# Float64 weights brought to two TensorE floats: a shift-and-or and a subtraction in place of three matrix products

## The chip, the cores and the metric

One core of a Trainium2 chip runs the kernel. The metric is device microseconds of one execution, on that core. [...] The other engines named here are VectorE (DVE), ScalarE (ACT), GpSimd (POOL) and SyncE (SP), whose queue issues all loads and stores.

## The reference, cut to what matters

```python
# attention: 8 batches, 8 heads, 576 positions, 64 per head
scores = where(0 <= rel < 128, q @ k.T / 8 + bias, -1e9)
x = softmax(scores) @ v                  # -> (8, 576, 512)
# gated layer: w_in (512, 1024), w_spatial (576, 576), w_out (512, 512)
h = maximum(x @ w_in, 0); u, v = halves(h)
v = layer_norm(v)
v_s = einsum('ts,bsd->btd', w_spatial, v) + b_spatial
out = (u * v_s) @ w_out
```

`w_in` and `w_out` arrive as float64, 8 bytes an element.

## The kernel before, in words

**The work.** Everything that follows is one program of one core, written out instruction by instruction. Attention of the first batch is done in fp32: `raw_tile` (scores of one 128-query tile of a head pair, and their exponentials), `raw_sums`, `raw_out` (scaling, transposes on TensorE, product with v). Attention of the batches 1 to 7 is done per head pair by `products` (P), `scores` (C), `values_split` (V) and `attention` (A). The gated layer of a batch has 5 v units (four of 128 positions and a remainder, `v_rem`), 8 u units, 8 s units (the spatial product) and 8 o units (the output product), each of 8 to 14 matmuls into one of two PSUM banks, tag "m". Nearly all TensorE time goes to these units; each factor stands as a high and a low part, so a product is three matmuls.

**The weights.** A 128-row piece of `w_in` has two halves of 512 columns: half 1 feeds the v units, half 0 the u units. With four pieces each, and four of `w_out`, 12 pieces go through `split_w64` (L386). A piece is loaded as int32 pairs, low and high word. L399 (ACT) takes the high word's absolute value as a float, L403 clamps it, L407 shifts its exponent and upper 20 fraction bits into the fp32 place, L411 puts sign and top exponent bit back: the result `x` holds the upper 20 fraction bits. `copy` makes the high part, an fp32r cast of `x`. L419 cuts the power of two out of `x`, and L423 multiplies the low word, as an unsigned number, by it. For the eight pieces of `w_in` (`WPE` True) TensorE then forms `x` minus high minus (minus low word) with three products by a unit matrix and by its negative (`ident`, `minus`; L441, L442, L443) in a bank of tag "m", and a second `copy` takes that to the low part. For `w_out` (`WPE` False) two DVE operations, L431 and L435, do the same. Each `split_w64` has two scratch tiles, of tag "gs" or "vraw".

**The order.** `record` adds units to a `Plan`; `copy`, `relu` and some scalings may go to ACT or DVE, the rest names its engine. The plan works out an order from weights, due times and data, and writes it out, so each engine has one fixed order in which it waits for what it needs. The string `OPENING` sets in which order the first units are recorded, and so who waits for which buffer: `a` and `w` are the pieces of half 1 and half 0, `z` those of `w_out`, `X`, `x`, `Y`, `y`, `g` the spatial weights, `t`, `m`, `n` batch 0's attention, `L`, `P`, `C`, `V`, `A` later attention, `v`, `u`, `s`, `o` the gated layer. 64 matmuls on a tile of ones (L362) run in between at the start.

**The place that matters below.** The first s unit needs all v parts of batch 0 (L910 and, of the remainder, L940). After the first two s units both "m" banks are taken until L979 has multiplied an s result into u.

Of the kernel before, what the change touches and what calls it, by code (L numbers as in the profile page):

```python
# [26 lines left out]
CLAMP = _as_f32((1150 << 20) | 0xFFFFF)  # L27
TINY = _as_f32(897 << 20)
# [165 lines left out]
def attn_gmlp_kernel(ctx, tc, qk, v, w_in, w_spT, b_sp, w_out, outT):  # L194
# [9 lines left out]
    DM, DF = w_in.shape  # L204
    DH = DF // 2
# [10 lines left out]


    WTMP = ("vraw", 3)
    WPE = (True, True, False)
    OPENING = (  # L220
# [40 lines left out]
    def pe(*cols):  # L261
        return sum(12 + n / 2.38 for n in cols)
# [27 lines left out]

    rstat = fixed([P, 2, 4, 2 * NP], F32, "rstat")
    ident = fixed([P, P], F32, "ident")
    minus = fixed([P, P], F32R, "minus")

    def parts(b, a, z, step=P, key=()):

# [12 lines left out]
    def constants():  # L309
# [35 lines left out]

        def f():
            nc.vector.tensor_scalar(ident(), diag()[:, :P], 0.0, None, ALU.is_equal)
            nc.vector.tensor_scalar(minus(), ident(), -1.0, None, ALU.mult)
        plan.add("DVE", 290, 500, f, [(diag, 0)], [(ident, 0), (minus, 0)])
# [36 lines left out]
    def split_w64(src, dst, tmp, hi, lo, due, on_pe, late=()):  # L386

        n = src[1]  # L390
        ta, tx = tmp
        low = lambda: src[0]()[:, :, 0]
        high = lambda: src[0]()[:, :, 1]
        a, x, ai, xi = ta, tx, lambda: ta().bitcast(I32), lambda: tx().bitcast(I32)
        part, PART = (late[0], (late[0], 0)) if late else (lo, (dst[0], (*dst[1], 1)))
        A, X, W, HI, LO = (ta, 0), (tx, 0), (src[0], 0), (dst[0], (*dst[1], 0)), (dst[0], (*dst[1], 1))

        def f():
            nc.scalar.activation(a(), high().bitcast(F32), AF.Abs)  # L399
        plan.add("ACT", act(n) + 100, due, f, [W], [A])  # L400

        def f():
            nc.vector.tensor_scalar(a(), a(), TINY, CLAMP, ALU.max, ALU.min)  # L403
        plan.add("DVE", dve(n, True), due, f, [A], [A])

        def f():
            nc.vector.tensor_scalar(xi(), ai(), 0x07FFFFFF, 3, ALU.bitwise_and, ALU.logical_shift_left)  # L407
        plan.add("DVE", dve(n, True), due + 1, f, [A], [X])
# [4 lines left out]
        def top():  # L413
            copy(n, lambda: (hi(), x()), due + 3, [X], [HI], fast=True)
        if on_pe and not late:
            top()

        def f():
            nc.vector.tensor_scalar(ai(), xi(), -0x800000, None, ALU.bitwise_and)  # L419
        plan.add("DVE", dve(n, True), due + 4, f, [X, A], [A])  # L420

        def f():
            nc.vector.scalar_tensor_tensor(part() if on_pe else a(), low().bitcast(U32), -2.0 ** -52 if on_pe else 2.0 ** -52, a(),  # L423
                                           ALU.mult, ALU.mult)
        plan.add("DVE", dve(n), due + 5, f, [A, W], [PART] if on_pe else [A])
        if late or not on_pe:
            top()
        if not on_pe:

            def f():  # L430
                nc.vector.tensor_tensor(x(), x(), hi().bitcast(F32), ALU.subtract)  # L431
            plan.add("DVE", dve(n), due + 6, f, [X, HI], [X])

            def f():
                nc.vector.tensor_tensor(lo(), x(), a(), ALU.add)  # L435
            plan.add("DVE", dve(n), due + 7, f, [X, A], [LO])
            return
        pt = plan.buf(ps, "m", 2, [P, 512], F32)

        def f():  # L440
            nc.tensor.matmul(pt()[:, :n], ident(), x(), start=True, stop=False)  # L441
            nc.tensor.matmul(pt()[:, :n], minus(), hi(), start=False, stop=False)  # L442
            nc.tensor.matmul(pt()[:, :n], minus(), part(), start=False, stop=True)  # L443
        plan.add("PE", pe(4 * n, n, n) + 130, due + 6, f, [PART, X, HI, (ident, 0), (minus, 0)], [(pt, 0)])
        copy(n, lambda: (lo(), pt()[:, :n]), due + 7, [(pt, 0)], [LO])

    def win_load(half, c, due, tag, bufs):
        st = plan.buf(work, tag, bufs, [P, DH, 2], I32)
# [670 lines left out]
```

## Time and profile before, and how to read it

| | |
|---|---|
| median of 3 runs | 565.38 us (562.99 to 565.69) |
| the profiled execution | span 563.3 us from its first to its last instruction; the page gives no other time of it |
| busy PE, DVE, ACT | 550.4 (98%), 463.5 (82%), 420.0 (75%) us |
| chain that ended last | PE 13% of the span, nothing else over 0.5% |
| L441, L442, L443 together | 24 product instructions on 8 pieces, between 16 and 65 us |
| POOL | 30.1 us busy (5%) |

The span of the profiled execution lies 2.1 us under the median and 0.3 us over the fastest run. A busy time is the union of an engine's instructions; successive instructions of DVE and ACT overlap by a little in the records, so what one costs its queue is the time from its start to the next one's start.

### The profile page before, as it was taken

To read this page: it belongs to the slowest core of one execution; us is meant where nothing else is said; L and a number is where in the kernel's file an instruction comes from. 1 tells how busy PE (TensorE), PEld (TensorE's weight loads), DVE (VectorE), ACT (ScalarE), POOL (GpSimd) and SP (SyncE) were. 2 spreads that over 40 slices of the span, in tenths; PEclk is the share of its full clock that TensorE was granted. 3 is DMA by queue.
4 is the path that set the end of the run, shared out by engine and by line. 5 is a ranking of instruction groups with operands and counts; after the bars stand their busy time and mean duration, and the time that the engine had idled before them with its cause. 6 is when DMAs were issued, how large, how long until landed. Compare 5 with 4: busy or idle time off the path is not lost. (4 is left out here: it accounts for less than half of the span.)

```text
span 563.3 us, 16409 instructions
## 1 busy us (share of the span) xinstructions
PE 550.4 (98%) x6184; PEld 474.8 (84%) x6184; DVE 463.5 (82%) x1756; ACT 420.0 (75%) x1329; POOL 30.1 (5%) x75
## 2 busy tenths in 40 slices
PE   8999997999999999999999999999999999999997
PEld 4566786888989899998989989998989989888987
DVE  6999999999999999868988897989988898625340
ACT  5999985988898889757886775887977787634321
POOL 0000010000100010001100020001000010001000
PEclk8999998999999999999999999999999999999999
DMA  7937414877668857575167644487267523410002
GB/s 234 365 126 261 110 44 95 214 186 185 132 136 185 154 130 169 121 184 139 43 154 170 170 115 93 117 176 182 80 147 173 129 43 70 90 44 23 1 1 84
DMA packets 131028, 74.28 MB, mean 132 GB/s; under 512 B 109314, under 2 KB 121602, under 8 KB 130948
## 3 DMA queue, kind: packets, MB, share of 16 engines
q1 hardware_dynamic: 130948, 73.23, 52.8%
q8 instruction: 48, 0.79, 0.6%
q14 instruction: 32, 0.26, 0.2%
HBM read 37.13 MB, written 9.44 MB: 83 GB/s over the span
## 5 line engine op out<-in xcount | busy, mean ns | idle before, releaser
L971 PE MATMUL m<-wsp,vn 128*128 128x288 f16 x768 | 112.6, 289 | 0.0
L950 PE MATMUL m<-xt,win 128*128 128x288 f32 x768 | 110.6, 298 | 0.3
L715 ACT ACTIVATE prob<-prob,stat 128x192 f32<-128x192 f32 (+2 forms) x252 | 107.2, 430 | 2.9 <-DVE stat L709 2.7
L950 PEld LDWEIGHTS m<-xt,win 128*128 128x128 f32 x768 | 104.0, 188 | 2.9 <-ACT vt L383 0.8
L997 PE MATMUL m<-gs,wout 128*128 128x288 f32 x732 | 101.8, 297 | 0.0
L997 PEld LDWEIGHTS m<-gs,wout 128*128 128x128 f32 x732 | 97.9, 188 | 0.8 <-issue 0.2
L744 ACT ACTIVATE pq<-prob,stat 128x192 f16<-128x192 f32 (+2 forms) x252 | 90.0, 428 | 6.2 <-DVE stat L738 4.1
L899 PE MATMUL m<-win,xt 128*128 128x512 f32 x384 | 92.0, 393 | 0.1
L971 PEld LDWEIGHTS <-vn 128*128 128x128 f16 x768 | 72.6, 99 | 20.6 <-issue 0.2
L749 DVE SCALAR_TENSOR_TENSOR pq<-prob,stat,pq 128x192 f16<-128x192 f32 (+2 forms) x252 | 86.8, 390 | 2.5 <-ACT pq L744 2.3
L899 PEld LDWEIGHTS m<-win,xt 128*128 128x128 f32 x384 | 71.0, 188 | 15.3 <-issue 0.5
L709 DVE CUSTOM_DVE_ANT_0 prob<-s,tabs 128x192 f32<-128x192 f32 (+2 forms) x252 | 71.0, 330 | 3.0 <-PE s L695 2.8
L979 DVE SCALAR_TENSOR_TENSOR u<-m,rows,u 128x288 f32<-128x288 f32 x64 | 32.8, 514 | 25.0 <-PE m L971 24.2
L715 ACT ACTIVATION_READ_ACCUMULATOR prob<-prob,stat 128x1 f32 x252 | 48.3, 192 | 0.0
L695 PE MATMUL s<-qkraw 64*64 64x192 f32 (+1 forms) x1008 | 44.0, 310 | 0.0
L379 ACT CAST gs<-u 128x288 fp32r<-128x288 f32 x48 | 20.5, 426 | 30.3 <-DVE u L979 30.1
L827 PEld LDWEIGHTS <-vh 64*64 64x64 f16 x1232 | 34.7, 107 | 9.3 <-issue 6.2
L827 PE MATMUL x<-pt,vh 64*64 64x192 f16 (+2 forms) x1232 | 39.6, 224 | 1.8 <-POOL am L836 1.8
L873 POOL TENSOR_TENSOR st<-st,nhalf 128x1 f32<-128x1 f32 (+1 forms) x40 | 26.0, 649 | 235.1 <-DVE st L869 217.2
L695 PEld LDWEIGHTS s<-qkraw 64*64 64x64 f32 x1008 | 36.5, 133 | 1.8 <-issue 0.6
L848 ACT ACTIVATE xt<-x,am 128x320 fp32r<-128x320 f32 (+1 forms) x56 | 25.2, 494 | 16.6 <-PE x L827 16.5
L864 DVE BATCH_NORM_STATS2 st<-vt 128x6 f32<-128x512 f32 (+1 forms) x40 | 27.4, 685 | 9.6 <-ACT vt L383 9.6
(155 smaller groups left out, 777.1 us busy)
## 6 DMA issues: line engine op xcount, KB each, us to landing
qkraw<-in_qk_dram SPq DMA_DIRECT2D x28, 576.0 KB, 4.5
out_dram<-o SPq DMA_DIRECT2D x64, 144.0 KB, 2.1
vraw<-in_v_dram SPq DMA_DIRECT2D x28, 320.0 KB, 3.5
wout<-in_w_in_dram SPq DMA_DIRECT2D x4, 512.0 KB, 6.6
vn<-in_w_in_dram SPq DMA_DIRECT2D x4, 512.0 KB, 7.1
wout<-in_w_out_dram SPq DMA_DIRECT2D x4, 512.0 KB, 4.8
wraw<-in_w_spT_dram SPq DMA_DIRECT2D x4, 288.0 KB, 6.7
pt<-pq SPq DMA_TRANSPOSE x56, 4.3
```

What stands on the lines that cost most here:

```text
L695: nc.tensor.matmul(flat(bank)[rows, c0:c0 + n], raw()[j * D:(j + 1) * D, 0, i * D:(i + 1) * D], raw()[j * D:(j + 1) * D, 1, (i + 1) * D - ...
L709: nc.vector.tensor_tensor_reduce(pt(), flat(bank)[:, c0:c0 + n], tabs()[:, 2 * p + odd, W - n:], -0.125, 3e38, ALU.add, ALU.min, st()[:, N ...
L715: nc.scalar.activation(pt(), pt(), AF.Exp, bias=st()[:, NM, k:k + 1], scale=-1.0, accum_out=st()[:, SM, k:k + 1])
L744: nc.scalar.activation(pq()[:, qc:qc + n], prob()[:, pc:pc + n], AF.Copy, scale=st()[:, RC, k:k + 1])
L749: nc.vector.scalar_tensor_tensor(pq()[:, qc + PLANE:qc + PLANE + n], prob()[:, pc:pc + n], st()[:, RC, k:k + 1], pq()[:, qc:qc + n], ALU.m ...
L827: done.append(nc.tensor.matmul(xps[half]()[j * D:(j + 1) * D, x0:x0 + len(ks) * D], l()[rows, kb // 2, j * D:(j + 1) * D], ap, start=(half ...
L864: nc.vector.bn_stats(st()[:m, 0:6], vt()[:m])
L899: nc.tensor.matmul(pt(), xt[c]()[:, X0[a] + t * P:X0[a] + (t + 1) * P], win()[:, c, w, DH:DF], start=(n == 0), stop=(n == 3 * NC_ - 1))
L950: nc.tensor.matmul(pt()[:, :HS], win()[:, c, w, d * P:(d + 1) * P], xt[c]()[:, X0[a] + hf * HS:X0[a] + (hf + 1) * HS], start=(n == 0), sto ...
L971: nc.tensor.matmul(pt()[:, :HS], l, r, start=(n == 0), stop=(n == len(ops) - 1))
L979: nc.vector.scalar_tensor_tensor(u(), pt()[:, :HS], rows()[:, INV:INV + 1], u(), ALU.mult, ALU.mult)
L997: nc.tensor.matmul(pt()[:, :HS], wout[d]()[:, w, e * P:(e + 1) * P], gs[d]()[:, a, :], start=(n == 0), stop=(n == 3 * ND - 1))
```

## The change

`split_w64` no longer has two ways. The absolute value may go to ACT or DVE (on DVE an and with 0x7FFFFFFF). After the step that put sign and exponent in place, a new operation shifts the low word right by 29 and ors the three bits into `x`, which then has the upper 23 fraction bits. High is a cast of `x` as before, low is `x` minus high, one DVE subtraction. L419, L423, L431, L435, the three products, their bank and the copy out of it are gone, and so are `minus` and one scratch tile of the two. `OPENING` is a new string of the same units.

```diff
-    WPE = (True, True, False)
     OPENING = (
-        "w00 a03 t11 t01 t10 t03 t00 t02 m00 n00 t13 t12 m10 n01 n02 n03 t20 n11 a02 n10 t21 a00 X01 t22 t23 m20 n12 n22 "
...
+        "t10 t11 X03 t00 t01 t03 a03 t02 m00 n00 w00 t13 n01 n02 t12 t20 a02 m10 n11 n10 a00 n03 X01 t22 a01 t21 n12 t23 t31 "
...
-            nc.vector.tensor_scalar(minus(), ident(), -1.0, None, ALU.mult)
...
-        def f():
-            nc.scalar.activation(a(), high().bitcast(F32), AF.Abs)
-        plan.add("ACT", act(n) + 100, due, f, [W], [A])
...
+        def fa():
+            nc.scalar.activation(x(), high().bitcast(F32), AF.Abs)
+
+        def fv():
+            nc.vector.tensor_scalar(xi(), high(), 0x7FFFFFFF, None, ALU.bitwise_and)
+        plan.either([("ACT", act(n) + 100, fa), ("DVE", dve(n, True), fv)], due, [W], [X])
...
         def f():
             nc.vector.scalar_tensor_tensor(xi(), high(), -0x40000000, xi(), ALU.bitwise_and, ALU.bitwise_or)
         plan.add("DVE", dve(n), due + 2, f, [W, X], [X])
...
-            nc.vector.tensor_scalar(ai(), xi(), -0x800000, None, ALU.bitwise_and)
-        plan.add("DVE", dve(n, True), due + 4, f, [X, A], [A])
...
-            nc.vector.scalar_tensor_tensor(part() if on_pe else a(), low().bitcast(U32), -2.0 ** -52 if on_pe else 2.0 ** -52, a(),
-                                           ALU.mult, ALU.mult)
...
-                nc.vector.tensor_tensor(x(), x(), hi().bitcast(F32), ALU.subtract)
...
-                nc.vector.tensor_tensor(lo(), x(), a(), ALU.add)
...
-            nc.tensor.matmul(pt()[:, :n], ident(), x(), start=True, stop=False)
-            nc.tensor.matmul(pt()[:, :n], minus(), hi(), start=False, stop=False)
-            nc.tensor.matmul(pt()[:, :n], minus(), part(), start=False, stop=True)
-        plan.add("PE", pe(4 * n, n, n) + 130, due + 6, f, [PART, X, HI, (ident, 0), (minus, 0)], [(pt, 0)])
-        copy(n, lambda: (lo(), pt()[:, :n]), due + 7, [(pt, 0)], [LO])
+        def f():
+            nc.vector.scalar_tensor_tensor(xi(), low(), 29, xi(), ALU.logical_shift_right, ALU.bitwise_or)
+        plan.add("DVE", dve(n), due + 3, f, [W, X], [X])
+        copy(n, lambda: (hi(), x()), due + 4, [X], [HI], fast=True)
+
+        def f():
+            nc.vector.tensor_tensor(lo(), x(), hi().bitcast(F32), ALU.subtract)
+        plan.add("DVE", dve(n), due + 5, f, [X, HI], [LO])
```

In the changed kernel's own line numbers: L395 and L398 are the absolute value on ACT and DVE, L402, L406, L410 the three steps kept, L414 the new shift-and-or, L419 the subtraction, L376 any `copy`; L873, L895, L924, L945, L971 are the matmuls of the v, remainder, u, s and o units (before: L899, L921, L950, L971, L997), L669 those of P (L695), L884 and L914 the low v parts (L910, L940), L953 the multiplication into u (L979).

TensorE, the units ahead of the first s unit, before the change (`x` and `m` are banks, `xt` batch 0's attention output, `win` the parts of `w_in`):

```order
L647 MATMUL x_70<-pq,pt 64x64 x4
L441 MATMUL m<-gs,ident 128x512
L442 MATMUL m<-win,minus 128x512
L443 MATMUL m<-win,minus 128x512
L441 MATMUL m<-gs,ident 128x512
L442 MATMUL m<-win,minus 128x512
L443 MATMUL m<-win,minus 128x512
L899 MATMUL m<-win,xt 128x512 x24
L950 MATMUL m<-xt,win 128x288 x48
L921 MATMUL m<-win,xt 128x512 x8
```

The same place after it:

```order
L621 MATMUL x_70<-pq,pt 64x64 x4
L895 MATMUL m<-win,xt 128x512 x8
L873 MATMUL m<-win,xt 128x512 x24
L924 MATMUL m<-xt,win 128x288 x12
L669 MATMUL s_67<-qkraw 64x192 x2
```

The last two of the eight triples stood there; now the remainder (x8) and two v units follow at once. Ahead of the first s unit stand the same units in both: four v units, the remainder, six u units and three P.

DVE, the rows up to the last one that the first s unit needs, before the change (`l_1188` is the remainder's low part, `wout` parts of `w_out`, `wsp` the spatial weights):

```order
L864 BN_STATS st<-vt 64x6
L423 SCALAR_TENSOR_TENSOR vraw<-wout_718,vraw 128x512
L868 BN_AGGR st<-st 64x2
L869 TENSOR_SCALAR st<-st 64x1
L534 SCALAR_TENSOR_TENSOR wsp<-wraw_464,rows,wsp 128x576
L534 SCALAR_TENSOR_TENSOR wsp<-wraw_493,rows,wsp 128x576
L877 TENSOR_SCALAR vt<-vt,st 64x512
L431 TENSOR_TENSOR vraw<-vraw,wout_1179 128x512
L403 TENSOR_SCALAR vraw<-vraw 128x512
L940 TENSOR_TENSOR l_1188<-vt,l_1188 64x512
```

The same after it (`vn_1088` is the low part of the last v unit):

```order
L842 BN_AGGR st<-st 128x2
L843 TENSOR_SCALAR st<-st 128x1
L508 SCALAR_TENSOR_TENSOR wsp<-wraw_482,rows,wsp 128x576
L884 TENSOR_TENSOR vn_1066<-vt,vn_1066 128x512
L851 TENSOR_SCALAR vt<-vt,st 128x512
L402 TENSOR_SCALAR vraw<-vraw 128x512
L406 TENSOR_SCALAR vraw<-vraw 128x512 x2
L410 SCALAR_TENSOR_TENSOR vraw<-wout_703,vraw 128x512
L884 TENSOR_TENSOR vn_1088<-vt,vn_1088 128x512
```

The remainder's part came last and is now ahead of the others; the last v unit's part comes last, and the pieces of `w_out` (`vraw`) are at about the same step of their split.

## Rows read from the trace of the kernel before

**Rows 1.** Busy time of each engine by stretch (us, instructions), granted clock, DMA.

```profile
20.00:80.00 60.00, 58.67 (x513) 40.94 (x514) 58.68 (x230) 59.33 (x191) 2.67 (x4) 1.00 0.51 165
80.00:100.00 20.00, 16.91 (x160) 13.93 (x155) 19.27 (x61) 12.62 (x37) 0.99 (x1) 0.91 0.48 119
100.00:200.00 100.00, 98.67 (x1374) 87.09 (x1366) 95.65 (x390) 89.00 (x296) 5.07 (x16) 1.00 0.77 170
200.00:480.00 280.00, 279.85 (x3349) 251.87 (x3348) 244.43 (x936) 216.58 (x698) 17.17 (x41) 1.00 0.55 129
```

**Rows 2.** Timeline of PE, two triples and what follows: start, length, instructions.

```profile
40.45 1.12 PE L441 MATMUL m<-gs,ident 128*128 128x512 f32 x2
...
41.97 0.54 PE L590 MATMUL s<-qkraw 64*64 64x192 f32 x4
...
63.36 1.02 PE L441 MATMUL m<-gs,ident 128*128 128x512 f32 x2
...
64.68 5.63 PE L899 MATMUL m<-win,xt 128*128 128x512 f32 x24
```

**Rows 3.** Timeline of PE at the first two s units; in brackets a wait.

```profile
83.92 0.54 PE L971 MATMUL m<-wsp,vn 128*128 128x288 f16 x3
87.56 0.66 PE L971 MATMUL m<-r,l 128*128 128x288 f16 x2 [3.09 <-DVE l L940]
...
91.97 1.32 PE L950 MATMUL m<-xt,win 128*128 128x288 f32 x8
```

**Rows 4.** Timeline of DVE at the same place.

```profile
86.82 0.68 DVE L940 TENSOR_TENSOR l<-vt,l 64x512 f16<-64x512 f32 x1
...
90.42 0.52 DVE L979 SCALAR_TENSOR_TENSOR u<-m,rows,u 128x288 f32<-128x288 f32 x1
```

**Rows 5.** Waits of PE over the whole span: total, times, longest.

```profile
PE m L971 <- DVE l L940: 3.1, 1, 3.1
PE s L590 <- DMA qkraw<-in_qk_dram: 1.8, 2, 1.4
PE x L827 <- POOL am L836: 1.8, 6, 0.4
```

**Rows 6.** Timeline of DVE where steps of `split_w64` stand back to back.

```profile
14.14 0.42 DVE L379 CAST win<-gs 128x512 fp32r<-128x512 f32 x1
14.48 0.42 DVE L403 TENSOR_SCALAR gs<-gs 128x512 f32<-128x512 f32 x1
...
15.43 0.68 DVE L423 SCALAR_TENSOR_TENSOR win<-wout,gs 128x512 fp32r<-128x512 uint32 x1
16.03 0.69 DVE L411 SCALAR_TENSOR_TENSOR gs<-vn,gs 128x512 int32<-128x512 int32 x1
```

**Rows 7.** Timeline of DVE at a subtraction of `w_out`'s split.

```profile
58.48 0.69 DVE L431 TENSOR_TENSOR vraw<-vraw,wout 128x512 f32<-128x512 f32 x1
59.09 0.42 DVE L403 TENSOR_SCALAR vraw<-vraw 128x512 f32<-128x512 f32 x1
```

**Rows 8.** Groups by form, 0 to 100 us: count, busy, mean ns, idle before.

```profile
L379 ACT CAST win<-m 128x512 fp32r<-128x512 f32 x6 | 3.5, 577 | 0.0
...
L625 DVE TENSOR_SCALAR pt<-pt,rstat 128x192 f32<-128x192 f32 x10 | 3.0, 312 | 0.0
L399 ACT ACTIVATE gs<-wout 128x512 f32<-128x512 f32 x4 | 2.9, 723 | 0.6 <-DMA wout<-in_w_in_dram 0.6
...
L379 DVE CAST win<-m 128x512 fp32r<-128x512 f32 x2 | 1.4, 682 | 0.0
```

**Rows 9.** Busy time by stretch as in group 1, where the granted clock fell.

```profile
8.00:10.00 2.00, 1.48 (x17) 0.71 (x17) 0.59 (x4) 0.54 (x3) 0.00 (x0) 0.65 0.95 295
10.00:12.00 2.00, 2.00 (x20) 0.57 (x12) 1.22 (x11) 1.40 (x6) 0.00 (x0) 0.50 1.06 373
...
86.00:88.00 2.00, 0.44 (x2) 0.28 (x3) 1.94 (x4) 1.02 (x2) 0.00 (x0) 0.78 0.00 0
88.00:90.00 2.00, 2.00 (x10) 1.27 (x9) 2.00 (x9) 0.66 (x2) 0.00 (x0) 0.50 0.35 96
```

More of the change, by code (lines that the diff above doesn't have):

```diff
@@ L292, in attn_gmlp_kernel @@
     ident = fixed([P, P], F32, "ident")
-    minus = fixed([P, P], F32R, "minus")
     def parts(b, a, z, step=P, key=()):
@@ L347, in f @@
             nc.vector.tensor_scalar(ident(), diag()[:, :P], 0.0, None, ALU.is_equal)
-            nc.vector.tensor_scalar(minus(), ident(), -1.0, None, ALU.mult)
-        plan.add("DVE", 290, 500, f, [(diag, 0)], [(ident, 0), (minus, 0)])
+        plan.add("DVE", 150, 500, f, [(diag, 0)], [(ident, 0)])
         for k, (t, n, ap) in enumerate(((prob, 3, lambda: prob().rearrange("p (a n) -> p a n", n=512)[:, :, W:W + P]), (pt_prob, 4, lambda: pt_prob()[:, :, W:W + P]))):
@@ L384, in relu, with split_w64 @@
                      ("DVE", dve(n, fast), lambda: nc.vector.tensor_scalar(*ap(), 0.0, None, ALU.max))], due, reads, writes)
-    def split_w64(src, dst, tmp, hi, lo, due, on_pe, late=()):
+    def split_w64(src, dst, tmp, hi, lo, due):
         n = src[1]
-        ta, tx = tmp
+        x = tmp
         low = lambda: src[0]()[:, :, 0]
         high = lambda: src[0]()[:, :, 1]
-        a, x, ai, xi = ta, tx, lambda: ta().bitcast(I32), lambda: tx().bitcast(I32)
-        part, PART = (late[0], (late[0], 0)) if late else (lo, (dst[0], (*dst[1], 1)))
-        A, X, W, HI, LO = (ta, 0), (tx, 0), (src[0], 0), (dst[0], (*dst[1], 0)), (dst[0], (*dst[1], 1))
+        xi = lambda: x().bitcast(I32)
+        X, W, HI, LO = (x, 0), (src[0], 0), (dst[0], (*dst[1], 0)), (dst[0], (*dst[1], 1))
+        def fa():
[3 more added lines that the diff above has]
+        plan.either([("ACT", act(n) + 100, fa), ("DVE", dve(n, True), fv)], due, [W], [X])
         def f():
-            nc.scalar.activation(a(), high().bitcast(F32), AF.Abs)
-        plan.add("ACT", act(n) + 100, due, f, [W], [A])
+            nc.vector.tensor_scalar(x(), x(), TINY, CLAMP, ALU.max, ALU.min)
+        plan.add("DVE", dve(n, True), due, f, [X], [X])
         def f():
-            nc.vector.tensor_scalar(a(), a(), TINY, CLAMP, ALU.max, ALU.min)
-        plan.add("DVE", dve(n, True), due, f, [A], [A])
-        def f():
-            nc.vector.tensor_scalar(xi(), ai(), 0x07FFFFFF, 3, ALU.bitwise_and, ALU.logical_shift_left)
-        plan.add("DVE", dve(n, True), due + 1, f, [A], [X])
+            nc.vector.tensor_scalar(xi(), xi(), 0x07FFFFFF, 3, ALU.bitwise_and, ALU.logical_shift_left)
+        plan.add("DVE", dve(n, True), due + 1, f, [X], [X])
         def f():
@@ L412, in split_w64 @@
         plan.add("DVE", dve(n), due + 2, f, [W, X], [X])
[L413 to L416, printed above, removed]
         def f():
-            nc.vector.tensor_scalar(ai(), xi(), -0x800000, None, ALU.bitwise_and)
-        plan.add("DVE", dve(n, True), due + 4, f, [X, A], [A])
+            nc.vector.scalar_tensor_tensor(xi(), low(), 29, xi(), ALU.logical_shift_right, ALU.bitwise_or)
+        plan.add("DVE", dve(n), due + 3, f, [W, X], [X])
+        copy(n, lambda: (hi(), x()), due + 4, [X], [HI], fast=True)
         def f():
-            nc.vector.scalar_tensor_tensor(part() if on_pe else a(), low().bitcast(U32), -2.0 ** -52 if on_pe else 2.0 ** -52, a(),
-                                           ALU.mult, ALU.mult)
[L425 to L430, printed above, removed]
-                nc.vector.tensor_tensor(x(), x(), hi().bitcast(F32), ALU.subtract)
-            plan.add("DVE", dve(n), due + 6, f, [X, HI], [X])
-            def f():
-                nc.vector.tensor_tensor(lo(), x(), a(), ALU.add)
[L436 to L440, printed above, removed]
-            nc.tensor.matmul(pt()[:, :n], ident(), x(), start=True, stop=False)
-            nc.tensor.matmul(pt()[:, :n], minus(), hi(), start=False, stop=False)
-            nc.tensor.matmul(pt()[:, :n], minus(), part(), start=False, stop=True)
-        plan.add("PE", pe(4 * n, n, n) + 130, due + 6, f, [PART, X, HI, (ident, 0), (minus, 0)], [(pt, 0)])
-        copy(n, lambda: (lo(), pt()[:, :n]), due + 7, [(pt, 0)], [LO])
+            nc.vector.tensor_tensor(lo(), x(), hi().bitcast(F32), ALU.subtract)
+        plan.add("DVE", dve(n), due + 5, f, [X, HI], [LO])
     def win_load(half, c, due, tag, bufs):
@@ L456, in win_weights @@
         cs = slice(half * DH, (half + 1) * DH)
-        split_w64((st, DH), (win, (half, c)), [plan.buf(work, "gs", 5, [P, DH], F32) for _ in range(2)],
-                  lambda: win()[:, c, 0, cs], lambda: win()[:, c, 1, cs], due, WPE[half])
+        split_w64((st, DH), (win, (half, c)), plan.buf(work, "gs", 5, [P, DH], F32),
+                  lambda: win()[:, c, 0, cs], lambda: win()[:, c, 1, cs], due)
     def wout_weights(c, due):
@@ L466, in wout_weights @@
         w = wout[c] = plan.buf(work, f"wout{c}", 1, [P, 2, DM], F32R)
-        split_w64((st, DM), (w, ()), [plan.buf(work, *WTMP, [P, DM], F32) for _ in range(2)],
-                  lambda: w()[:, 0, :], lambda: w()[:, 1, :], due, WPE[2])
+        split_w64((st, DM), (w, ()), plan.buf(work, *WTMP, [P, DM], F32), lambda: w()[:, 0, :], lambda: w()[:, 1, :], due)
     BITS = 0x7F800000
```

12 rows, old and new, of the table OPENING are left out of this document.

## The prediction

> **What bounds the kernel now.** I read the shares by stretch first, because the change touches only the first 100 us [rows 1]. From 200 to 480 us PE is busy 279.85 of 280 us: there the kernel is bound by TensorE, and nothing of the change lies there. From 20 to 80 us three engines are full at once: PE 58.67, DVE 58.68 and ACT 59.33 of 60 us. From 80 to 100 us PE has 16.91 of 20, ACT 12.62, and only DVE is still full with 19.27. So the opening is a stretch with three limits, and freeing one engine of it gives nothing by itself. The waits of PE [rows 5] then say which limit ends last. Over the whole span PE waits once for long, 3.1 us for L940, DVE's last part for the first s unit; in the attention units it waits 1.8 us in all, for the turn that POOL passes on. The timeline shows the place [rows 3]: three matmuls of the first s unit at 83.92, then 3.09 us of idle, then the rest at 87.56. On DVE [rows 4] L940 runs from 86.82 to 87.50 and PE goes on 0.06 us later. After that PE does not wait for data again, except those 1.8 us; what lies behind 88 us is TensorE work that the change leaves as it is. So the question is how much earlier DVE brings the last part that the first s unit needs.
>
> **TensorE.** Eight triples of products go. One takes PE from 40.45 to 41.97, 1.52 us, and another from 63.36 to 64.68, 1.32 us [rows 2]; the eight lie between these, so 8 x 1.42 = 11.4 us go, all ahead of 65 us. All eight stand ahead of the first s unit. If nothing else changed, PE would come to that unit 11.4 us sooner and wait 3.1 + 11.4 = 14.5 us for the same L940. On its own this term is worth 0; it is covered by DVE, and it comes in only as far as DVE gets faster.
>
> **DVE up to the last part.** What an operation costs its queue I read from start to start. A one-source operation on 512 columns: 14.48 - 14.14 = 0.34 us. L423: 16.03 - 15.43 = 0.60 us, and L411 has the same length in the record, 0.69 to 0.68 [rows 6]. A subtraction, L431: 59.09 - 58.48 = 0.61 us [rows 7]. I count in both orders the DVE rows up to the last one that the first s unit needs: L940 before, the low part of the last v unit after (the order puts it there).
> Gone up to there: 11 L419 at 0.34 = 3.7; 11 L423 at 0.60 = 6.6; 5 L431 or L435 at 0.61 = 3.0; 2 copies out of the bank at 0.60 (0.68 with its overlap [rows 8]) = 1.2; 3 casts of the high part, now on ACT, at 0.34 = 1.0. Together 15.6 us.
> Moved off DVE or behind the place: about a dozen small rows (casts of the attention output, one relu, one memset, five scalings like L625, 0.31 us long [rows 8], less what overlaps), about 3.0 us.
> New up to there: 10 shift-and-or; I take 0.60, that of L411, which has the same two sources and reads the same strided words. 10 subtractions at 0.61 = 6.1. 5 absolute values, which the order puts on DVE, at 0.34 = 1.7. One L406 earlier than its like, 0.3. Together 14.1 us.
> The sum is 14.1 - 15.6 - 3.0 = -4.5 us: the last part is done at 87.50 - 4.5 = 83.0 us.
>
> **Is ACT in time?** Up to its last cast for the first s unit ACT loses five absolute values of about 0.7 us and six copies out of the bank of 0.58 us [rows 8], 7 us, and gets a few casts back; net about 5 us less. It does not take over as the limit, but has hardly more room than DVE.
>
> **From there on.** Before, DVE's first L979 starts at 90.42, 2.9 us behind the end of L940 [rows 4], and PE begins the next u unit at 91.97 [rows 3], after two s units. After, the order puts 3.5 us of DVE rows between the last part and L953, so that ends at about 83.0 + 3.5 + 0.5 = 87.0, and the u unit, which needs its bank, follows: 5.0 us earlier. From 100 to 200 us DVE is still at 95.65 of 100 [rows 1], so some of this may be given back at the first attention and o units. I take 4.5 us, the gain of the last part. The profiled span becomes 563.3 - 4.5 = 558.8. The page gives no other time of that execution; the median of the runs is 2.1 us over its span, so on the scale of the runs I predict 565.4 - 4.5 = 560.9 us.
>
> **The unknown prices.** No row has the absolute value on DVE. Its nearest rows are 0.34 (one source, dense) and 0.60 (L411, strided words); I take 0.34, because it has one source, and the other end costs 5 x 0.26 = 1.3 us. [...] The shift-and-or could be as short as 0.34 or as long as its whole record, 0.68: 2.6 us of gain to 0.8 of loss over ten. The first weight operation on DVE now waits for a load itself, where before ACT did, 0.6 us in all [rows 8]; no load is added, SP issues the pieces in a slightly other order, and a wait there costs 0 to 1.5 us, since it holds the queue. On the good side, DVE's idle 1.3 + 0.7 us between 20 and 100 us [rows 1] may shrink with a freer PE. So the gain lies between about 1 and 8 us.
>
> **The clock.** [...] I expect PE to be short of work ahead of the first s unit still, so a low stretch there remains, and count nothing for it.
>
> **Rivals.**
> 1. The products were the bound: PE, DVE and ACT were all held by PE's order, and all 11.4 us come out: 565.4 - 11.4 = 554.0. For it, PE's 58.67 of 60. Against it, DVE and ACT were as full, and the one long wait is for DVE. 0.06.
> 2. The gain is given back: the absolute value costs 0.60, the first loads hold DVE, and the first attention and o units then wait for DVE, which stays at 95.65 of 100. 4.5 - 1.3 - 1.5 leaves 1.7 us: 563.7, or, if the new order gains nothing over the old, 565.4. 0.24.
> 3. [...] 0.05. [...]
> 4. The change does not do what it says: the order shows no product and no fifth step left, so this has no chance of its own.
>
> **How the numbers follow.** The forecast, a gain of 3 to 7 us, has 0.65. A measurement of this kernel can tell about 0.5%, 2.8 us, from no change. Faster by more than that: the forecast and rival 1, 0.71, less a little at the edge, 0.69. Within it: rival 2 and that edge, 0.26. Slower: rival 3, 0.05. The range reaches from a gain of 8.5, between the bounds above and rival 1, to a gain of 0.6, inside rival 2: 556.9 to 564.8 us. It leaves out most of rival 1, rival 3 and the end of rival 2.
>
> **What would show it.** Right: no TensorE product at the split; PE waiting more between 20 and 80 us while DVE and ACT stay full; the first s unit's last matmuls at 83 to 84 us; the u unit behind the second s unit at about 87; shift-and-or near 0.60 and the absolute value near 0.34 from start to start; from 200 us on the same busy PE. Wrong: PE still full from 20 to 80 us with the first s unit at 76 (rival 1); the first s unit at 86 or later (rival 2); a granted clock under 0.9 from 20 to 80 us (rival 3); waits of PE of more than 2 us in all between 88 and 200 us.

## The result and the profile after

The changed kernel takes 557.75 us (median of 4 runs, 557.59 to 558.21), the kernel before 565.15 in the same comparison: a ratio of 0.9874, 95% interval 0.9854 to 0.9893, 7.4 us less. The prediction was 560.9, from 556.9 to 564.8: the time lies in the range, the gain 0.4 us past the forecast 3 to 7 us and 2.9 over its single figure of 4.5. The profiled span is 556.4 us in place of 563.3.

Busy time by stretch in the changed kernel (columns as in [rows 1]):

```profile
20.00:80.00 60.00, 51.79 (x476) 37.80 (x476) 58.96 (x212) 57.58 (x180) 3.51 (x5) 0.97 0.57 178
80.00:100.00 20.00, 19.75 (x234) 17.71 (x233) 19.85 (x78) 17.82 (x60) 0.10 (x1) 1.00 0.68 138
100.00:200.00 100.00, 99.15 (x1302) 87.56 (x1301) 93.98 (x384) 89.40 (x295) 6.33 (x17) 1.00 0.73 163
200.00:480.00 280.00, 279.66 (x3392) 251.15 (x3390) 243.28 (x929) 216.43 (x697) 14.93 (x39) 1.00 0.59 129
```

Against [rows 1]: from 20 to 80 us PE has lost 6.9 us of work, VectorE is as full as before, ScalarE has 2.4 us free. From 80 to 100 us PE is now full. From 200 us on nothing has changed.

The first two s units on PE, and VectorE around the last part that they need (start, length, instruction, as in [rows 3, 4]):

```profile
80.80 1.49 PE L924 MATMUL m<-xt,win 128*128 128x288 f32 x10
82.13 0.54 PE L945 MATMUL m<-wsp,vn 128*128 128x288 f16 x3
82.51 0.41 PE L945 MATMUL m<-r,l 128*128 128x288 f16 x2
...
85.48 3.61 PE L924 MATMUL m<-xt,win 128*128 128x288 f32 x24
```

```profile
80.74 0.69 DVE L884 TENSOR_TENSOR vn<-vt,vn 128x512 f16<-128x512 f32 x1
...
84.88 0.48 DVE L953 SCALAR_TENSOR_TENSOR u<-m,rows,u 128x288 f32<-128x288 f32 x1
```

Three readings. The last part ends at 80.74 + 0.69 = 81.43, in place of 87.50, and PE no longer waits for it: it reaches the products that use l (the low part of the remainder, the first matmuls that waited before) at 82.51 in place of 87.56, **5.05 us earlier**. From there to the u unit before took 91.97 - 87.56 = 4.41 us, with the granted clock (a share of the full one) at 0.50 from 87.12 to 90.53 us [rows 3, 9]; now it takes 85.48 - 82.51 = 2.97, at a granted 1.00 and with no hold before the u unit, **1.44 us less**. That is 6.49 us at the u unit, of 6.9 in the span. So the gain is made up by 85.48 us, and little of it is given back.

Part of the 5.05 us may be the clock too. The kernel before has a low stretch (granted 0.50) from 8.61 to 12.02 us [rows 9]; the record of the changed kernel has a granted 1.00 in its first 20 us:

```profile
0.00:20.00 20.00, 15.92 (x164) 10.43 (x164) 15.62 (x83) 15.09 (x54) 1.02 (x7) 1.00 0.86 284
```

In a run of the old order without a low stretch there (all three cuts, below) the scores of batch 0 that come at 14.78 us in the kernel before come at 13.87, so an estimate of the share is up to 0.9 us. The times of single executions say how much the clock makes up in all. In one comparison the kernel before ran 27 times: the ten executions with a mean granted clock of 0.994 took 564.7 to 566.0 us (median 565.5), the three with 1.000 took 562.8 to 563.6. The three of the changed kernel with 0.999 or 1.000 took 557.6 to 557.8. So at the full clock some 5.4 us of the 7.4 are left; the lowest times of the main comparison, 562.99 and 557.59, lie as far apart. By this estimate some 2 us are the clock's. It is a rough one: in other comparisons four of five executions of the kernel before with a recorded 0.998 or 0.999 took 566.0 to 566.7, the fifth 562.9.

PE's waits over the whole span (total, times, longest), the longest sums:

```profile
PE x L621 <- ACT pq L376: 1.8, 2, 1.0
PE x L801 <- POOL am L810: 1.7, 6, 0.3
PE s L564 <- DVE gs L398: 1.4, 1, 1.4
PE m L606 <- ACT pt L598: 1.1, 2, 0.9
```

The one wait of 3.1 us [rows 5] is gone, shorter ones of up to 1.4 us have come. By PE's rows: its busy time falls from 550.4 to 538.6 us, its idle time up to the last matmul grows from 9.3 to 14.1 (overlaps taken out). Of 11.8 us taken off PE 4.8 came back as idle time.

### The profile page after: what moved, and what is told of

The parts are those of the page before. It is cut to its first block, busy times and chain, and to the rows that moved or that the text cites. A ratio compares the mean times of both kernels' runs of the same rounds, so it can differ in the third digit from the quotient of the medians.

```text
span 556.4 us, 16328 instructions
## 1 busy us (share of the span) xinstructions
PE 538.6 (97%) x6152; PEld 470.1 (84%) x6152; DVE 456.8 (82%) x1734; ACT 420.3 (76%) x1334; POOL 29.1 (5%) x75
## 5 line engine op out<-in xcount | busy, mean ns | idle before, releaser
L924 PE MATMUL m<-xt,win 128*128 128x288 f32 x768 | 110.5, 298 | 1.1 <-ACT vt L380 0.9
L945 PE MATMUL m<-wsp,vn 128*128 128x288 f16 x768 | 111.3, 287 | 0.0
L924 PEld LDWEIGHTS m<-xt,win 128*128 128x128 f32 x768 | 103.9, 188 | 4.0 <-ACT vt L380 2.2
L971 PE MATMUL m<-gs,wout 128*128 128x288 f32 x732 | 102.5, 297 | 0.0
L971 PEld LDWEIGHTS m<-gs,wout 128*128 128x128 f32 x732 | 98.1, 188 | 0.9
L873 PE MATMUL m<-win,xt 128*128 128x512 f32 x384 | 92.3, 393 | 0.8 <-DVE vt L904 0.8
L723 DVE SCALAR_TENSOR_TENSOR pq<-prob,stat,pq 128x192 f16<-128x192 f32 (+2 forms) x252 | 87.9, 389 | 2.7 <-ACT pq L718 2.5
L945 PEld LDWEIGHTS <-vn 128*128 128x128 f16 x768 | 72.0, 98 | 19.7
L873 PEld LDWEIGHTS m<-win,xt 128*128 128x128 f32 x384 | 71.0, 188 | 16.1 <-DVE vt L904 1.2
L953 DVE SCALAR_TENSOR_TENSOR u<-m,rows,u 128x288 f32<-128x288 f32 x64 | 32.9, 515 | 29.4 <-PE m L945 28.5
L669 PE MATMUL s<-qkraw 64*64 64x192 f32 (+1 forms) x1008 | 45.4, 316 | 1.0 <-DVE stat L683 1.0
L376 ACT CAST gs<-u 128x288 fp32r<-128x288 f32 x47 | 20.1, 427 | 30.8 <-DVE u L953 30.5
L669 PEld LDWEIGHTS s<-qkraw 64*64 64x64 f32 x1008 | 37.5, 136 | 3.1 <-DVE stat L683 1.9
```

The lines of the kernel that those rows point to most:

```text
L669: nc.tensor.matmul(flat(bank)[rows, c0:c0 + n], raw()[j * D:(j + 1) * D, 0, i * D:(i + 1) * D], raw()[j * D:(j + 1) * D, 1, (i + 1) * D - ...
L723: nc.vector.scalar_tensor_tensor(pq()[:, qc + PLANE:qc + PLANE + n], prob()[:, pc:pc + n], st()[:, RC, k:k + 1], pq()[:, qc:qc + n], ALU.m ...
L873: nc.tensor.matmul(pt(), xt[c]()[:, X0[a] + t * P:X0[a] + (t + 1) * P], win()[:, c, w, DH:DF], start=(n == 0), stop=(n == 3 * NC_ - 1))
L924: nc.tensor.matmul(pt()[:, :HS], win()[:, c, w, d * P:(d + 1) * P], xt[c]()[:, X0[a] + hf * HS:X0[a] + (hf + 1) * HS], start=(n == 0), sto ...
L945: nc.tensor.matmul(pt()[:, :HS], l, r, start=(n == 0), stop=(n == len(ops) - 1))
L953: nc.vector.scalar_tensor_tensor(u(), pt()[:, :HS], rows()[:, INV:INV + 1], u(), ALU.mult, ALU.mult)
```

## The experiments

Each ratio is to the kernel before in the same comparison, with its 95% interval. Where a run is set against the changed kernel, medians of two comparisons are subtracted; by the ratios these differences are up to 0.6 us smaller. TensorE is PE in the rows, VectorE DVE, ScalarE ACT, GpSimd POOL.

**Order and split apart.** The first run is the kernel before with only the new table:

```
-        "w00 a03 t11 t01 t10 t03 t00 t02 m00 n00 t13 ...
+        "t10 t11 X03 t00 t01 t03 a03 t02 m00 n00 w00 ...
```

> The split of before, products and all, in the new order of the first units. Theory A (DVE's work up to the first s unit is what counts; the changed kernel has 4.9 us less of it and 1.2 us less idle there): only idle time can go, so 0 to 2 us faster than before, about 564. Rival B (the new order is what pays): about 558, nearly all of the 7.4 us. Rival C (TensorE's products were the bound): no gain, 565, since the products are still there.

The second is the changed kernel with the old table (the same lines the other way round):

> The new split in the order of before. Theory A: the 4.9 us of DVE work go, the idle time of the old order stays or grows a little, so 3 to 5 us faster than before, 560 to 562. Rival B (order): 564 to 565. Rival C (products): 7 us or more faster, 558 or less, as the products are gone whatever the order.

Measured: the order alone 578.43 us, 1.0229 (1.0192 to 1.0267), 12.6 us **slower**; the split alone 565.81, 1.001 (0.999 to 1.0031). Every expectation for the first is missed; the second lies 0.8 us above rival B's 564 to 565, but that rival wanted 558 of the first. The split alone at the first s unit:

```profile
82.36 0.53 PE L945 MATMUL m<-wsp,vn 128*128 128x288 f16 x3
86.02 0.66 PE L945 MATMUL m<-r,l 128*128 128x288 f16 x2 [3.13 <-DVE l L914]
86.47 3.09 PE L945 MATMUL m<-wsp,vn 128*128 128x288 f16 x12
...
91.80 0.39 PE L924 MATMUL m<-xt,win 128*128 128x288 f32 x1
```

The part comes 87.56 - 86.02 = 1.54 us earlier, PE waits as long as before, and the two s units then take 91.80 - 86.02 = 5.78 us in place of 4.41, since more of them lies at the low clock (granted 0.50 from 84.94 to 91.77): 1.37 us lost. So what the split alone is ahead at l it gives back at PE's clock. Even the 1.54 us need not be the split's: its scores of batch 0 already came 1.84 us earlier (at 12.94), with no low clock there, and from them to l it takes 73.1 us, the kernel before 72.8. With the new order alone, no engine is full:

```profile
20.00:80.00 60.00, 50.92 (x413) 33.24 (x412) 54.94 (x213) 54.97 (x176) 0.85 (x2) 0.91 0.53 161
...
64.00:68.00 4.00, 1.98 (x25) 1.30 (x19) 3.97 (x11) 4.00 (x14) 0.00 (x0) 0.50 0.00 0
```

PE waits 3.29 us for VectorE ahead of 62.79 us, and has the low clock (0.50) from 62.94 to 73.18. The table suits the new split only.

What the two do to VectorE shows up to the end of the last low v part that the first s units need (in us; the last row is one of the cuts told below, in the old order):

| run | VectorE's work up to it | idle up to it | part done |
|---|---|---|---|
| before | 80.9 | 6.6 | 87.50 |
| split alone | 78.1 | 7.9 | 85.96 |
| order alone | 85.2 | 10.3 | 95.55 |
| changed kernel | 76.0 | 5.4 | 81.43 |
| before, VectorE cut | 75.9 | 10.9 | 86.72 |

With the split alone the plan sets more of the later attention ahead of that part (14 rows of L723, where the changed kernel has 9 and the kernel before 10), so 2.9 us of work go and 1.3 us of idle time come. With the table 4.9 us of work go, and 1.2 us of idle time with them. In the cut, with every engine's order kept, 5.1 us of work go and 4.3 us come back as idle time.

**Time put back on PE, time added on VectorE.** Two runs on the changed kernel, its order kept. The first puts fp32 products of 512 and 256 columns, about as long as a triple (1.39 us at 37.12, 1.49 at 39.10), ahead of 8 of batch 0's value products:

```
+            if t in (1, 2):
+                nc.tensor.matmul(xp()[:, :512], ident(), pf(0, 512), ...)
+                nc.tensor.matmul(xp()[:, :256], ident(), pf(0, 256), ...)
             for j in range(2):
```

> The changed kernel with TensorE work put back: ahead of eight of batch 0's products with v, matmuls of the length of a triple (an fp32 product of 512 columns and one of 256, some 1.3 us) whose result is overwritten; nothing else moves. Theory A: TensorE has 8.2 of 60 us free from 20 to 80 us, so the 10 us added cost 0 to 3 us, 558 to 561. Rival C (products): about 10 us, 566 to 568.

The second runs every shift-and-or twice:

```
             nc.vector.scalar_tensor_tensor(xi(), low(), 29, xi(), ...)
+            nc.vector.scalar_tensor_tensor(xi(), low(), 29, xi(), ...)
```

> The changed kernel with each shift-and-or done twice, which changes no value; 12 DVE operations of 0.60 us more, 10 of them ahead of the last part for the first s unit, in the same order. Theory A: the first s unit's last part comes 6 us later, and 5 to 7 us are lost, 563 to 565. Rival C: DVE is not what ends last, 0 to 2 us, 558 to 560.

Measured: 568.95 us, 1.0065 (1.0042 to 1.0087), 11.2 over the changed kernel; and 566.19, 1.0013 (0.9997 to 1.0029), 8.4 over it. (In the second's profiled execution a u unit's matmul took 937 ns on average, in place of 298 in the changed kernel's, and the span was 2485.7 us, so of its trace only the lengths of VectorE's rows are used.) Both miss what theory A gave. The first looks as if PE's time counted in full, but its waits say where the time went: from 20 to 60 us

```profile
DVE xt L376 <- PE x L624: 4.0, 4, 1.3
```

```profile
ACT xt L376 <- PE x L624: 5.6, 4, 2.3
```

VectorE and ScalarE stood 9.6 us for the very units that had the products in front of them; in the changed kernel it is 0.4 us. The triples of the kernel before stood ahead of other work. So this run shows what a delay in batch 0's chain costs, not what the triples cost where they were. The second:

```profile
102.62 0.68 DVE L414 SCALAR_TENSOR_TENSOR gs<-wout,gs 128x512 int32<-128x512 int32 x1
103.34 0.69 DVE L415 SCALAR_TENSOR_TENSOR gs<-wout,gs 128x512 int32<-128x512 int32 x1
103.95 0.35 DVE L574 CUSTOM_DVE_ANT_0 prob<-s,tabs 128x192 f32<-128x192 f32 x1
```

The pair takes 103.95 - 102.62 = 1.33 us, where one takes 0.60. 12 x 0.73 = 8.8 us of VectorE work added cost 8.4 us, by the ratios 7.9: nearly all of it.

**Cuts on PE and VectorE in the kernel before.** Three runs with the order of every engine unchanged: two of three products left out of each triple; the clamp and the mask of each split on one column; both.

```
-            nc.tensor.matmul(pt()[:, :n], ident(), x(), start=True, stop=False)
-            nc.tensor.matmul(pt()[:, :n], minus(), hi(), start=False, stop=False)
-            nc.tensor.matmul(pt()[:, :n], minus(), part(), start=False, stop=True)
+            nc.tensor.matmul(pt()[:, :n], minus(), part(), start=True, stop=True)
```

```
-            nc.vector.tensor_scalar(a(), a(), TINY, CLAMP, ...)
+            nc.vector.tensor_scalar(a()[:, :1], a()[:, :1], TINY, CLAMP, ...)
...
-            nc.vector.tensor_scalar(ai(), xi(), -0x800000, None, ...)
+            nc.vector.tensor_scalar(ai()[:, :1], xi()[:, :1], -0x800000, None, ...)
```

> The kernel before with two of each triple's three products left out (the one of the lower part stays, so each triple is 0.40 us in place of 1.52; 8 x 1.12 = 9.0 us of PE work less), every instruction of every engine otherwise in the order of before, VectorE and ScalarE with the same work; the lower parts that it computes lack two of their three terms. Theory A, of the prediction (the products are covered; rows of VectorE pace the opening): 564 to 566 us, and PE's idle time before 92 us grows by about 9. Theory B (PE's own work is what bounds the opening): 556 to 558. Theory C (PE and VectorE wait for one another in turn along one chain, so that a step of either lengthens it in part): 559 to 563.

> The kernel before with the clamp and the mask of each split on 1 column in place of 512 (24 VectorE operations of about 0.34 us that become about 0.07: some 6.5 us of VectorE work less), same order, PE as before; weights are not clamped or masked beyond the first column. Theory A: the last part of the first s unit comes 5 to 6 us earlier, 559 to 561 us. Theory B: 564 to 566, VectorE waits longer for PE. Theory C: 561 to 563.

> Both cuts at once: 9.0 us of PE work and some 6.5 us of VectorE work less in the order of before (the two parts of the computation that the two runs with one cut leave out). Theory A: as with the cut on VectorE alone, 558.5 to 561 us. Theory B: as with the cut on PE alone, 555.5 to 558. Theory C: more than the two single gains together, 551 to 556.

Measured: PE cut 567.81 us, 1.0044 (1.0024 to 1.0065); VectorE cut 563.79, 0.9965 (0.9946 to 0.9983); both 566.28, 1.0002 (0.9985 to 1.002). Less work on PE made the kernel slower. Its profile, 34 to 38 and 68 to 72 us (of the slowest of its eight executions, 570.17 us):

```profile
34.00:36.00 2.00, 2.00 (x23) 1.26 (x22) 2.00 (x11) 2.00 (x6) 0.00 (x0) 0.58 0.00 0
36.00:38.00 2.00, 2.00 (x12) 1.54 (x10) 1.09 (x4) 1.58 (x7) 0.00 (x0) 0.56 0.00 0
68.00:70.00 2.00, 1.78 (x5) 1.40 (x6) 1.94 (x12) 1.98 (x10) 0.00 (x0) 0.62 1.11 208
70.00:72.00 2.00, 2.00 (x7) 1.59 (x6) 2.00 (x13) 2.00 (x8) 0.55 (x1) 0.53 0.93 177
```

Two falls of the granted clock, to 0.56 and 0.53 in the lower 2 us of each, which the kernel before does not have (1.00 from 20 to 80 us [rows 1]); the first follows a wait of PE of 1.93 us:

```profile
33.24 0.66 PE L632 MATMUL m<-ident,pt 128*128 128x128 f32 x4 [1.93 <-ACT pt L624]
33.83 0.69 PE L647 MATMUL x<-pq,vraw 128*64 128x128 f32 x8
34.45 0.92 PE L590 MATMUL s<-qkraw 64*64 64x192 f32 x8
```

Since the order is that of before, each instruction can be set against itself: the lag behind the kernel before goes from 2.77 us (at 30.48) to 4.21 (at 33.48, 37.69 here), and from 3.54 (64.68) to 5.23 (67.88). About 1.5 us a fall. This execution was already 3.11 us behind at the scores of batch 0, so the profile overstates the loss; but the other executions point the same way: the median of the mean granted clock is 0.987 over the eight, 0.994 over the 24 of the kernel before in this comparison. The theories fall all three: neither engine alone is the bound (A, B), and the two cuts together give no more than one (C). ScalarE, which none of the three relieves, was as full as the others in the kernel before.

**Subtractions on GpSimd** in the changed kernel, order kept:

```
-            nc.vector.tensor_tensor(lo(), x(), hi().bitcast(F32), ALU.subtract)
+            nc.gpsimd.tensor_tensor(lo(), x(), hi().bitcast(F32), ALU.subtract)
```

> The changed kernel with the 12 subtractions of its splits on GpSimd in place of VectorE (12 x 0.61 to 0.68 us = 7.6 us of VectorE work less), same order on every other engine. If VectorE's rows pace the opening of the changed kernel too and GpSimd answers in time (theory A): 551 to 554 us. If PE bounds it by now (theory B): 556.5 to 558. If GpSimd's operation takes so long, or holds VectorE's so much, that the consumers of the lower parts wait: 559 to 566.

Measured: 562.31 us, 0.9945 (0.9926 to 0.9965), 4.6 over the changed kernel, as the third case had it. GpSimd, and VectorE beside it:

```profile
36.91 1.27 POOL L419 TENSOR_TENSOR win<-gs,win 128x512 fp32r<-128x512 f32 x1 [7.64 <-ACT win L376]
39.41 1.27 POOL L419 TENSOR_TENSOR win<-gs,win 128x512 fp32r<-128x512 f32 x1 [1.22 <-ACT win L376]
```

```profile
37.34 0.96 DVE L599 TENSOR_SCALAR pt<-pt,rstat 128x192 f32<-128x192 f32 x1
...
39.57 0.28 DVE L629 TENSOR_TENSOR xt<-x,xt 128x128 fp32r<-128x128 f32 x1
39.78 1.45 DVE L414 SCALAR_TENSOR_TENSOR gs<-wout,gs 128x512 int32<-128x512 int32 x1
```

In the changed kernel the same L599 takes 0.32 us and L414 0.69. So GpSimd needs 1.27 us where VectorE needs 0.61, and eleven of VectorE's operations between tiles in SBUF that start meanwhile take longer in this run, though not every one (a BATCH_NORM_STATS2 at 80.40 us keeps its 0.69), while L629, which reads the bank x, keeps its 0.28. VectorE's busy time is 459.7 us, above the 456.8 with the subtractions on it. Part of the loss is PE's clock, which is low (0.87 in the mean from 20 to 60 us) from 29.64 to 36.47 and from 43.29 to 46.70 us in this execution, the slowest of five (563.94).

**Cuts on ScalarE, in the kernel before**, order kept: batch 0's exponential on one column; with VectorE's cut; with all three.

```
-OUTSIDE = 2.0 ** 40
+OUTSIDE = 200.0
...
-                nc.scalar.activation(pr(), pr(), AF.Exp, ...)
+                nc.scalar.activation(pr()[:, :1], pr()[:, :1], AF.Exp, ...)
```

> The kernel before with the exponential of the first attention (36 calls on ScalarE, 0.44 to 0.50 us by their rows at 128 x 192) on 1 column in place of 192 or 128: some 6 to 9 us of ScalarE work less in the opening, same order, VectorE and PE as before (the attention is left without its exponential, and the mask's constant is 200 so that all numbers stay small). Theory A (rows of VectorE alone pace the opening): 564 to 566 us. Theory D (new: VectorE and ScalarE pace it together, both without idle time from 20 to 80 us in the kernel before, so a cut on one of them is lost in waits for the other): 562 to 565, ScalarE idle in its place. If ScalarE alone paces it: 557 to 560.

> The cut on ScalarE and that on VectorE (clamp and mask on 1 column) at once, PE as before, same order. Theory D: the last part of the first s unit 4 to 7 us earlier and 557 to 561 us, more than the two single gains together. Theory A: as with VectorE's cut alone, 562 to 565. If PE, which was busy for 98% of 20 to 80 us, now holds both (theory B): 561 to 565, and VectorE and ScalarE wait for PE.

> The three cuts at once (ScalarE, VectorE, and two of three products of each triple on PE), same order. Theory D with PE free of a part: at or below the run with the two cuts, 553 to 560 us; if PE's clock falls in the gaps that open on it, a stretch at half clock costs 1 to 2 us each and the run stands up to 5 us above the one with the two cuts. Theory B: 551 to 556 us, since now all three have room.

Measured: 565.47 us, 1.0004 (0.9983 to 1.0025); 563.87, 0.9977 (0.9956 to 0.9998); 562.97, 0.9969 (0.995 to 0.9988). The ScalarE cut was over-rated: 3.8 us by the busy time (420.0 to 416.2); VectorE's is 5.5 (463.5 to 458.0). The cut on ScalarE alone lies in theory A's range, 0.5 us above D's; the two cuts lie in those of A and B, 2.9 us above D's. The three cuts at once end 0.9 us below the two, which the intervals do not separate, and above the 560 of theory D and the 556 of theory B.

The table sets the six cuts side by side, each by its one profiled execution. Idle is 60 us less the busy time from 20 to 80 us. "Opening" runs from one row of PE, the scores of batch 0 at 14.78 us in the kernel before, to the product that waits for l (87.56 before), so that what happens at the very start stays out; "s units" from there to the u unit (91.97 before).

| run | idle PE, VectorE, ScalarE | falls of the clock, 20 to 80 us | opening | s units |
|---|---|---|---|---|
| before | 1.3, 1.3, 0.7 | 0 | 72.8 | 4.41 |
| PE cut | 7.5, 3.3, 2.6 | 2 | 74.6 | 4.58 |
| VectorE cut | 0.9, 4.5, 0.5 | 0 | 71.4 | 4.65 |
| PE and VectorE | 6.2, 6.0, 2.0 | 2 | 73.0 | 4.61 |
| ScalarE cut | 1.2, 1.5, 3.4 | 0 | 72.4 | 3.35 |
| VectorE and ScalarE | 0.8, 4.2, 2.9 | 0 | 71.1 | 3.35 |
| all three | 4.8, 3.5, 3.3 | 1 | 70.1 | 4.65 |

With one or two engines cut, an engine that is left uncut is idle for 3.3 us at most, mostly for less than 2, and the opening gains 0.4 to 1.7 us or loses. Only with all three cut is there more than 3 us of room on each, and it gains 2.7, less than any of the cuts, with a fall of the clock in it. No engine is then full, and PE still waits 2.6 us for l. That the chain of waits in the old order is what remains is likely, but not shown.

The last column shows the clock alone. With ScalarE cut, PE waits as long as before, yet the clock does not fall (granted 1.00 from 80 to 100 us, where the kernel before has 0.91 [rows 1]):

```profile
85.49 0.54 PE L971 MATMUL m<-wsp,vn 128*128 128x288 f16 x3
89.15 0.42 PE L971 MATMUL m<-r,l 128*128 128x288 f16 x2 [3.12 <-DVE l L940]
...
92.50 3.55 PE L950 MATMUL m<-xt,win 128*128 128x288 f32 x24
```

92.50 - 89.15 = 3.35 us, against 4.41 to 4.65 in the five with a fall there. So the fall costs 1.1 to 1.3 us at this place, and VectorE's L979 hides only a part of it: in this run it ends at 92.44 and holds PE until then. Of the 1.44 us in the changed kernel 4.41 - 3.35 = 1.06 is then the clock, and 3.35 - 2.97 = 0.38 that the u unit starts without a hold.

**The same cuts in the changed kernel**, order kept: the exponential, and the clamp and the masking step on one column.

```
-            nc.vector.tensor_scalar(xi(), xi(), 0x07FFFFFF, 3, ...)
+            nc.vector.tensor_scalar(xi()[:, :1], xi()[:, :1], 0x07FFFFFF, 3, ...)
```

> The changed kernel with the cuts of the run on ScalarE and VectorE (the exponential of the first attention on 1 column with the mask's constant at 200; the clamp and the masking step of each split on 1 column, 24 VectorE operations of about 0.34 us), every instruction in the order of the changed kernel, PE's work as there; the attention is left without its exponential and the weights' high parts unclamped and unmasked. In the kernel before the same cuts gave 1.3 us of 565.2, with 0.8 us of idle time left on PE from 20 to 80 us. Theory F (VectorE, ScalarE and PE were all three full in the kernel before, so that any two could be relieved for nothing; the change took from all three, and left PE 8.2 us idle there): here the same cuts give 3 to 6 us, 552 to 555 us, and PE's idle time from 20 to 80 us falls to 3 to 5 us. Theory G (the order and its chains of waits hold the opening, whatever is free): 556 to 558 us, VectorE and ScalarE idle in place of the cut work. A fall of PE's clock in a gap that opens would add 1 to 2 us to either.

Measured: 555.14 us, 0.983 (0.9805 to 0.9855), 2.6 us under the changed kernel by the medians; the span is 3.2 shorter. By instruction it is 0.1 us ahead at 16.7, 2.4 at 44.8, 3.1 at 51.5 and 3.1 at the first s unit.

```profile
20.00:80.00 60.00, 52.40 (x492) 38.81 (x491) 57.52 (x217) 56.56 (x183) 3.50 (x5) 1.00 0.55 178
```

The time lies between the two theories, 0.1 us above F's range and 0.9 below G's, and what F named as its mark is missing: PE's idle time from 20 to 80 us goes from 8.2 to 7.6 us only, not to 3 to 5. In the opening the cuts gave 1.7 us in the old order and 3.0 here (the lead at the first s unit less that at 16.7): a little more room, with most of the work cut still turning into waits. Whether PE's room makes that difference stays open.

## Why the prediction was right or wrong

**"Freeing one engine of it gives nothing by itself"** was nearly right, and the prediction should have held on to it. Shown by the cuts: PE alone 1.0044, ScalarE alone 1.0004, VectorE alone 0.9965, which is 2 us for 5.5 us of work.

**TensorE, "on its own this term is worth 0"**: right in size. "It is covered by DVE" is not: with VectorE cut as well the ratio is 1.0002. Three engines cover one another.

**VectorE up to the last part, "-4.5 us", part done at 83.0.** This is the step that failed, as reasoning more than as a number. The part was done at 81.43, 6.1 us earlier. By the same rows VectorE's work up to it went from 80.94 to 76.03 us, 4.9 less, near the 4.5, and its idle time from 6.56 to 5.39. So the count of rows was good, and the term that was missing is the idle time: the step took VectorE's sum as the time itself, and gave no reason why its waits should stay as they were. They do not. With the order kept, 5.1 us of VectorE work less came back as 4.3 us of idle time, and the split alone added 1.3 us of it. What the runs put in its place: in the opening the split relieves PE, VectorE and ScalarE at once, and the order makes the relief usable; split alone 1.001, order alone 1.0229, both 0.9874. That the sum came out near is in part luck: of the orders that ran it holds only in the one in which the idle time does not grow. How the table achieves that, unit by unit, was not taken apart.

**Is ScalarE in time?** It is; up to the last part its work fell from 77.13 to 73.88 us, 3.3 where 5 was expected.

**"From there on"**: 3.5 us of VectorE rows between the part and L953 were expected; L953 starts at 84.88, 3.45 after 81.43. The expected loss of 0.5 us behind it is not there: 6.49 us at the u unit are 6.9 in the span.

**The prices** held. Start to start in the changed kernel:

```profile
38.69 0.42 DVE L398 TENSOR_SCALAR gs<-wout 128x512 int32<-128x512 int32 x1
39.03 0.28 DVE L629 TENSOR_TENSOR xt<-x,xt 128x128 fp32r<-128x128 f32 x1
...
45.25 0.68 DVE L414 SCALAR_TENSOR_TENSOR gs<-wout,gs 128x512 int32<-128x512 int32 x1
45.85 0.68 DVE L419 TENSOR_TENSOR win<-gs,win 128x512 fp32r<-128x512 f32 x1
46.46 0.69 DVE L838 BATCH_NORM_STATS2 st<-vt 128x6 f32<-128x512 f32 x1
```

The absolute value costs 39.03 - 38.69 = 0.34, the shift-and-or 0.60, the subtraction 0.61. The absolute value, with a single 4-byte source that is read with a stride, kept the 0.34 of the dense cast [rows 6]. The wait for a load came at its upper end:

```profile
10.09 0.43 DVE L398 TENSOR_SCALAR gs<-vn 128x512 int32<-128x512 int32 x1 [1.47 <-DMA vn<-in_w_in_dram]
```

PE then waits 1.42 us behind it, at 10.57. It is inside the 0 to 1.5 that were given.

**The clock, "a low stretch there remains, and count nothing for it"**: the second step that failed, and a term of the sum that was missing. The stretch is gone: PE reaches l after it is ready, and the granted clock is 1.00 from 80 to 100 us. The two s units take 1.44 us less, 1.06 of it by the clock. No run shows the nothing that was counted for such a stretch: where the clock stayed full behind the same wait, the same matmuls took 3.35 us in place of 4.41 to 4.65, and VectorE's L979 did not hold PE in [rows 3, 4]: it ended at 90.42 + 0.52 = 90.94, and PE began the u unit at 91.97. The low stretch of 8 to 12 us is gone too; with it the clock's share is an estimated 2 us of the 7.4, by the executions at the full clock. One fall appears elsewhere in the changed kernel:

```profile
52.00:54.00 2.00, 1.74 (x16) 1.39 (x20) 2.00 (x11) 2.00 (x9) 0.00 (x0) 0.56 0.03 8
54.00:56.00 2.00, 2.00 (x34) 1.71 (x27) 2.00 (x8) 1.98 (x7) 0.00 (x0) 0.58 0.01 4
```

As far as one run can show, it costs nothing that lasts: the last run has no fall there, and is as far ahead behind it (3.1 us at 57.8) as in front of it.

**The rivals.** 1 is out: the first s unit begins at 82.13, not at 76. 2 is out: the 6.49 us at the u unit were kept. 3, the slower kernel, did not happen: the ratio is 0.9874, and the granted clock from 20 to 80 us is 0.97, above the 0.9 of its mark. But the clock can take back what PE is spared, as the PE cut shows: PE is idle for 7.5 us from 20 to 80 us in place of 1.3, its clock falls two times more in the opening, and each fall costs about 1.5 us.

So of the 6.9 us in the span 5.05 come from an earlier l and 1.44 from quicker s units, mostly the clock, where the prediction had 4.5 and 0. Up to some 0.9 of the 5.05 may be the clock at the start. Both terms were too small, and in the same direction; the wide range held the error.

## What to carry to other kernels

Where several engines are full at once, one engine's sum of work is no forecast by itself: 8.8 us of work added to VectorE cost 8.4 here, 5.5 us taken off it alone gave 2 (0.35% of 565), and a change has to be weighed with the order in which it runs. Find the wait that ends the stretch and ask what the clock does behind it: with TensorE work taken away the clock fell two times more here, at about 1.5 us each (the PE cut, ratio 1.0044), and with a wait of 3.09 us removed the u unit behind it came 6.49 us earlier. Count an engine's idle time up to the place that matters beside its work. A table of order found for one set of costs can be worth less than nothing with another: here it cost 12.6 us.

## What the runs showed of the hardware

- Beside GpSimd's subtraction of two tiles in SBUF (1.27 us for 128 x 512) eleven of VectorE's operations between tiles in SBUF took longer in that run: 0.96 us for 0.32, 1.45 for 0.69. A BATCH_NORM_STATS2 kept its 0.69, and an operation that reads a bank of PSUM its 0.28.
- The same wait of 3.1 us on PE came with a fall of the granted clock to 0.50 in the kernel before (87.12 to 90.53 us) and with none when ScalarE was cut (1.00 from 80 to 100 us), nearly the same program: 4.41 and 3.35 us for the same matmuls.
- At the start the clock differs from run to run with nearly the same program up to there: the same scores of batch 0 came at 13.9 us (all three cut, no low stretch), 14.8 (the kernel before, granted 0.50 from 8.61 to 12.02), 16.8 (ScalarE cut, 8.80 to 15.63) and 17.9 (the PE cut). The last has a granted clock of 1.00 there, yet 21 products on the tile of ones took 4.12 us (first line) in place of 2.47 in the kernel before (second): in this run the record of the clock does not show what the lengths do.

```profile
13.84 4.12 PE L362 MATMUL x<-ones 128*128 128x256 bf16 x21
```

```profile
12.39 2.47 PE L362 MATMUL x<-ones 128*128 128x256 bf16 x21
```

- Executions of one and the same kernel differ with it: 562.8 to 563.6 us at a mean granted clock of 1.000, 564.7 to 566.0 at 0.994 (the kernel before).
